# Finer places per expert in a fused attention and top-1 expert kernel: token counts rounded to 8 instead of 32

## The chip, the cores and the metric

The kernel runs on one core of a Trainium2 chip. A core has five engines that run side by side and wait for each other by semaphores: TensorE (PE in the profile; PEld is its loading of weights), VectorE (DVE), ScalarE (ACT), GpSimd (POOL) and SyncE (SP, which here only starts transfers). The metric is the time of one execution on the device in microseconds. A time is the median of several executions; before the change it is 478.34 us (three runs, 477.48 to 478.46).

## The reference

A block of decayed linear attention makes x of 3072 tokens by 512 numbers. Then each token goes to one of 8 experts, the one with the largest logit, and that expert's two-layer network gives the output row:

```python
logits = x @ w_gate
expert_idx = np.argmax(logits, axis=1)
probs = np.exp(logits - logits.max(-1, keepdims=True)); probs /= probs.sum(-1, keepdims=True) + 1e-09
gate_w = probs[np.arange(N), expert_idx]
for e in range(E):
    mask = expert_idx == e
    h = np.maximum(x[mask] @ w1[e], 0.0)              # w1[e]: 512 x 1024
    out[mask] = gate_w[mask, None] * (h @ w2[e])      # w2[e]: 1024 x 512
```

All numbers are fp32. Which token goes where is known only on the device, once its logits are there.

## The kernel before, in words

**Attention and lists.** The first part (to about 137 us) computes x in blocks of 128 tokens, writes it to a table `xs` in HBM, picks each token's expert, and writes an entry (row in `xs`, row of the output, gate) into the next free place of that expert's list in HBM (`put`, L370 to L395).

**Places.** The work for an expert is laid out before the counts are known, so it gets a fixed number of places, `CAPS`. Places that no token takes hold an entry that reads a row that counts for nothing and whose output row is skipped. Expert 0 comes first; the other seven follow in order of their counts, largest first, which the device finds out at run time (L730 to L764). This text calls them rank 1 to rank 7. `CAPS` before is three tiles of 128 and a fourth of `LASTS`: 416, 448, 416, 416, 384, 384, 384, 384. Should an expert have more tokens than places, a loop at the end (L805 to L823), behind a condition, runs further tiles with that expert's weights loaded anew.

**Passes.** `make_pass` (L405) lays out one pass: its tile widths (`m.widths`), and the load of its list. There are nine. Expert 0 has two: 0a, its first 256 places, started before attention ends, and 0b, the rest. Then one for each rank. A pass has these steps:

- `fetch` (L428): GpSimd gathers the tokens' rows, one indirect transfer a tile (L436).
- `turn` (L460): TensorE transposes the tiles, four chunks of 128 features each (L465), and VectorE and ScalarE copy them out of PSUM (L452, L450). A tile of w tokens is a transpose with w rows in and w columns out.
- First layer. Passes 0a and 0b use `hidden` (L470): 32 matmuls (L475) whose moving operand is all the pass's tokens at once. The ranks use `hidden_fast` (L542), a form of Strassen's product: the tokens are cut into two halves of h = n/2, and 56 matmuls (L551) each stream h columns; sums of halves are formed on VectorE (L488 to L492, L560) and ScalarE. `token_sums` (L534) and `first_sums`, `second_sums` (on GpSimd, L512 and L515) form the operands' sums ahead of time.
- Second layer. `outputs_fast` (L572) makes tiles 0 and 1 together in the same form (L579), and leaves the third and fourth tiles to `outputs` (L598): eight matmuls of 512 columns (L609), where a tile narrower than 128 is cut into k = 128 / w column groups of TensorE's array, each writing its own range of PSUM partitions; VectorE adds the groups' partial sums (L613 to L618).
- `scatter` (L440): GpSimd writes the rows to their places in the output.

**Order.** The loop at L777 issues, for each pass, its first layer, then the transposes and sums of the pass behind it, then its outputs. The gather of the pass after next is issued there too, and waits until a transpose has freed its buffer; the next weights are loaded once a buffer of weights is free. On every engine instructions run in the order in which they stand.

Of the kernel before, what the change touches and what calls it, by code (L numbers as in the profile page):

```python
# [20 lines left out]
def kernel(  # L21
# [29 lines left out]
    nc = tc.nc  # L51
    B, H, S, D = q.shape
    N, MD = out.shape
    E = moe_w_gate.shape[1]
    F = moe_w1.shape[2]
    P = 128
# [3 lines left out]
    DC = MD // P  # L60
    FC = F // P


    TG = 3
    NR = E - 1
    LASTS = [32, 64, 32, 32, 0, 0, 0, 0]
    CAPS = [TG * P + last for last in LASTS]

    TE = 2
    EARLY = TE * P  # L70
# [2 lines left out]
    R = N + EARLY + P  # L73
    ENTRY = 4

    MORE = -((TG * P - N - EARLY) // P)

    const = ctx.enter_context(tc.tile_pool(name="const", bufs=1))
    dram = ctx.enter_context(tc.tile_pool(name="dram", bufs=1, space=DRAM))
# [66 lines left out]
    for i in range(E):  # L146
        nc.vector.memset(caps[:, i:i + 1], float(CAPS[i]))

# [9 lines left out]
    for h in itertools.chain(range(0, H, 2), range(1, H, 2)):  # L158
        nc.vector.tensor_tensor_scan(
            out=decay[:, h % 2, h // 2, :], data0=lam_bc[:, h:h + 1].to_broadcast([P, C]),  # L160
# [11 lines left out]
    def pick(per_e, e):  # L172

        if isinstance(e, int):
            return per_e[e]
        return per_e[bass.ds(e, 1)].squeeze(0)

    def load_weights(e):
        w1t = wpool.tile([P, DC, F], F32, tag="w1", name="w1t")
        nc.sync.dma_start(out=w1t, in_=pick(w1_r, e))  # L180
        w2t = wpool.tile([P, FC, MD], F32, tag="w2", name="w2t")
        nc.sync.dma_start(out=w2t, in_=pick(w2_r, e))
        return w1t, w2t
# [11 lines left out]
    def bank(i, shape, name):  # L195
        return ps.tile(shape, F32, tag=f"bank{i}", name=name)
# [7 lines left out]
    def pin(inst):  # L204
        tc.keep_in_program_order(inst)
# [196 lines left out]
    NT = TG + 1  # L402
    by_e = slots.rearrange("(e r) c -> e r c", e=E)

    def make_pass(e, r0, tiles, last, name):  # L405

        m = SimpleNamespace(tiles=tiles, last=last, widths=[P] * tiles + [last] * (last > 0))
        src = by_e[e] if isinstance(e, int) else by_e[bass.ds(e, 1)].squeeze(0)
        m.n = sum(m.widths)
        nt = len(m.widths)  # L410
        m.list = ffn.tile([P, NT, ENTRY], F32, name=f"list_{name}", bufs=1)
        nc.sync.dma_start(
            out=m.list[:, :nt, :],
            in_=src[r0:r0 + nt * P, :].rearrange("(t p) c -> p t c", t=nt))
        m.ids = m.list.bitcast(I32)
        m.w = e
        return m

    def at(m, t):

        w = m.widths[t]
        return m.ids[:w, t, 0:1], m.ids[:w, t, 1:2], m.list[:w, t, 2:3]
# [5 lines left out]
    def fetch(m, rows=1 + N):  # L428
        m.xg = []
        for t, w in enumerate(m.widths):  # L430
            if t % 2 == 0:
                m.xg.append(ffn.tile([P, 2, MD], F32, tag="xg", name="xg", bufs=2))
            gather(m.xg[-1][:w, t % 2, :], at(m, t)[0], rows)
# [6 lines left out]
    def scatter(idx, src):  # L440

        put = nc.gpsimd.indirect_dma_start(  # L442
            out=out, out_offset=bass.IndirectOffsetOnAxis(ap=idx, axis=0), in_=src,
            in_offset=None, bounds_check=N - 1, oob_is_err=False)
        tc.declare_no_dep(put.ins, group="rows", reason="a token is on one list, once")
        tc.add_to_no_dep_group("rows", put.ins)
# [13 lines left out]
    def turn(m, pin=lambda inst: inst):  # L460
        m.xgT = ffn.tile([P, DC, m.n], F32, tag="xgT", name="xgT", bufs=1)
        for dc in range(DC):
            tp = bank(next(tp_banks), [P, m.n], "tp")
            for t, w in enumerate(m.widths):
                pin(nc.tensor.transpose(tp[:, t * P:t * P + w],  # L465
                                        m.xg[t // 2][:w, t % 2, dc * P:(dc + 1) * P],
                                        ident[:w, :w]))
            evac(dc, m.xgT[:, dc, :], tp)

    def hidden(m, w1t):  # L470
        m.hT = ffn.tile([P, FC, m.n], F32, tag="hT", name="hT", bufs=1)
        for fc in range(FC):
            ph = bank(next(ph_banks), [P, m.n], "ph")
            for dc in range(DC):
                nc.tensor.matmul(ph, lhsT=w1t[:, dc, fc * P:(fc + 1) * P], rhs=m.xgT[:, dc, :],  # L475
                                 start=(dc == 0), stop=(dc == DC - 1))
            relu(fc, m.hT[:, fc, :], ph)
# [120 lines left out]
    def outputs(m, w2t, tiles=None):  # L598
        for t in tiles or range(len(m.widths)):
            w = m.widths[t]  # L600


            k = P // w
            _, idx, gate = at(m, t)
            po = bank(next(po_banks), [P, MD], "po")

            for i, fc in enumerate((0, 1, 4, 5, 2, 3, 6, 7)):
                part = slice(i % k * w, (i % k + 1) * w)
                nc.tensor.matmul(po[part], lhsT=m.hT[:, fc, t * P:t * P + w], rhs=w2t[:, fc, :],  # L609
                                 start=(i < k), stop=(i >= FC - k), skip_group_check=True)  # L610
            o = ffn.tile([P, MD], F32, tag="o", name="o", bufs=4)
            if t % 2 or k > 1:
                nc.scalar.activation(o[:w], po[:w], ACT.Copy, scale=gate)  # L613
            else:
                nc.vector.tensor_scalar_mul(o[:w], po[:w], gate)  # L615
            for j in range(1, k):
                nc.vector.scalar_tensor_tensor(out=o[:w], in0=po[j * w:(j + 1) * w], scalar=gate,
                                               in1=o[:w], op0=ALU.mult, op1=ALU.add)  # L618
            scatter(idx, o[:w])

# [27 lines left out]
    def enter(n, b):  # L648
        if n + 1 < NSTEP:
            loaded[n + 1, b] = load(n + 1, b)  # L650
        if (n, b) == (NSTEP - 2, B - 2):
            weights.append(load_weights(0))
        m = SimpleNamespace(n=n, b=b, qT=[], qsT=[], kT=[], kd=[], mt=[], xT=[])
        m.q, m.k, m.v = loaded[n, b]

        for s, turn_one in (((0, turn_q), (1, turn_q), (0, turn_k), (1, turn_k)) if not (n or b)
                            else ((0, turn_q), (0, turn_k), (1, turn_q), (1, turn_k))):
            turn_one(m, s)
        return m
# [3 lines left out]
    def give_places(group):  # L663
        put(*group)
        if group[:2] == early:
            start_early()
# [15 lines left out]
    passes = []  # L682
    skip = const.tile([P, 1], F32, name="skip")

    def start_early():

        had = bank(5, [P, E], "had")
        pin(nc.tensor.matmul(had, lhsT=ones, rhs=acc_early, start=True, stop=True))
        nc.vector.tensor_scalar(out=skip, in0=had[:, 0:1], scalar1=-1.0, scalar2=float(EARLY),
                                op0=ALU.mult, op1=ALU.add)  # L690
        nc.vector.tensor_scalar_max(skip, skip, 0.0)
        base[0] = const.tile([P, E], F32, name="ebase_late")
        nc.vector.tensor_copy(base[0], ebase)
        nc.vector.tensor_add(base[0][:, 0:1], base[0][:, 0:1], skip)
        m = make_pass(0, 0, TE, 0, "0a")
        fetch(m, 1 + ((NSTEP - 2) * B + CUT) * C)
        passes.append(m)

    order = [(n, b) for n in range(NSTEP) for b in range(0, B, 2)]
    cur, last = enter(*order[0]), None  # L700
    for s in range(2):
        score(cur, s)
    for i in range(len(order)):
# [19 lines left out]
        last, cur = cur, ahead  # L723
# [35 lines left out]
    beyond = const.tile([P, E + 1], I32, name="beyond")  # L759
# [4 lines left out]
    nc.vector.tensor_reduce(out=beyond[:, E:], in_=beyond[:, :E], axis=AX.X, op=ALU.max)  # L764


    passes.append(make_pass(0, EARLY, TG - TE, LASTS[0], "0b"))
    for i in range(1, E):
        e = nc.values_load(turns[0:1, i:i + 1], min_val=1, max_val=E - 1,
                           engines=[mybir.EngineType.SP])  # L770
        passes.append(make_pass(e, 0, TG, LASTS[i], str(i)))
        if i == 1:
            weights.append(load_weights(e))
    for m in passes[1:3]:
        fetch(m)
    last = len(passes) - 1
# [25 lines left out]
            weights.append(load_weights(passes[i + 2].w))  # L802


    most = nc.values_load(beyond[0:1, E:E + 1], min_val=0, max_val=MORE)  # L805
    with tc.If(most > 0):
        for i in range(E):
            tiles = nc.values_load(beyond[0:1, i:i + 1], min_val=0, max_val=MORE)
            with tc.If(tiles > 0):
                e = i  # L810
                if i > 0:
                    e = nc.values_load(turns[0:1, i:i + 1], min_val=1, max_val=E - 1)
                w1t, w2t = load_weights(e)
                with tc.For_i(0, tiles, 1) as r:
                    m = SimpleNamespace(n=P, widths=[P])
                    m.list = ffn.tile([P, 1, ENTRY], F32, tag="list", name="list")
                    m.ids = m.list.bitcast(I32)
                    nc.sync.dma_start(
                        out=m.list[:, 0, :], in_=pick(by_e, e)[bass.ds(r * P + CAPS[i], P), :])
                    fetch(m)  # L820
                    turn(m)
                    hidden(m, w1t)
                    outputs(m, w2t)  # L823
# [28 lines left out]
```

## Time and profile before

| what | value |
|---|---|
| median of three runs | 478.34 us |
| the profiled execution | 478.98 us |
| its span, first to last instruction | 477.2 us |
| granted TensorE clock, mean | 0.997 |
| TensorE busy | 457.3 us, 96% |
| of it: L609, L551's first group, L579's first group | 81.1, 42.8, 26.8 us |
| share of L551, L579, L609, L475, L465 in the chain that ended last | 28%, 18%, 16%, 5%, 3% |
| VectorE, ScalarE, GpSimd busy | 47%, 27%, 52% |

How to read it: the page describes one execution. An engine's busy time is the union of its instructions. An fp32 matmul of the program leaves two records, so 56 matmuls of L551 are "x112". The chain that ended last is followed back from the last instruction, at each step to what released it. In a group, `128*128 128x192` is a weight tile of 128 rows by 128 columns against a moving operand of 128 rows by 192 columns, then follow the count, the busy time, the mean of one in ns, and the idle time before them with what ended it. A matmul's own duration holds its way through the array and overlaps the next, so the price of one in a stream is read from the chain: the length of a piece over its count.

### The profile page before, as it was taken

What the parts mean: (1) busy time and instruction counts of PE and PEld (TensorE: products, weight loads), DVE (VectorE), ACT (ScalarE), POOL (GpSimd) and SP (SyncE); (2) the same over time, 40 slices, a digit from 0 to 9 for tenths busy, and PEclk for the clock granted to TensorE, in tenths of its full rate; (3) what the DMA queues carried; (4) which work ended last, traced back from release to release, by engine and by line L of the source; (5) the groups of instructions that cost most, each with busy time, mean ns of one, the idle gap of its engine ahead of it and who ended that gap; (6) DMA issues with size and microseconds to landing.
All of it is one profiled execution on the core that took longest, in us unless ns stands there. A gap on an engine that the chain in (4) does not pass through costs nothing.

```text
span 477.2 us, 8695 instructions
## 1 busy us (share of the span) xinstructions
PE 457.3 (96%) x3468; PEld 383.1 (80%) x3468; DVE 224.4 (47%) x525; ACT 127.0 (27%) x323; POOL 247.7 (52%) x189
## 2 busy tenths in 40 slices
PE   4799999999899999999999999999999999999994
PEld 3789999998686677957994898699699689779963
DVE  3657758585450134452345436434524623753421
ACT  3364445544320111222131122113112212211310
POOL 5423644524335829849806951991694497711001
PEclk9999999999999999999999999999999999999998
DMA  9999999999318557060506152351633615001001
GB/s 170 240 243 260 217 239 216 257 305 279 101 47 320 157 193 250 32 243 33 208 13 242 36 212 87 157 199 47 243 110 132 233 39 211 0 19 44 1 17 51
DMA packets 99856, 72.84 MB, mean 153 GB/s; under 512 B 81226, under 2 KB 81230, under 8 KB 99808
## 3 DMA queue, kind: packets, MB, share of 16 engines
q1 hardware_dynamic: 88688, 51.97, 39.2%
q0 software_dynamic: 5008, 13.41, 7.8%
q10 hardware_dynamic: 6112, 6.83, 4.3%
q8 instruction: 29, 0.48, 0.5%
q14 instruction: 19, 0.16, 0.1%
HBM read 59.13 MB, written 13.40 MB: 152 GB/s over the span
## 4 chain that ended last, share of the span: by engine, by line
PE 71%; issue 3%; DVE 1%; DMA 1%; POOL 0%; POOLq 0%; ACT 0%
PE p L551 28%; PE p L579 18%; PE po L609 16%; PE ph L475 5%; PE tp L465 3%; DMA xg<-xs,list_0a 1%; DVE h_qsT L498 0%; DVE hT L560 0%; PE tx L326 0%; POOL slots L390 0%; PE tx L328 0%; DVE xgT L452 0%; PE rank L377 0%; POOLq L805 0%; ACT hT L562 0%
## 5 line engine op out<-in xcount | busy, mean ns | idle before, releaser
L609 PE MATMUL po<-w2t,hT 128*128 128x512 f32 (+2 forms) x224 | 81.1, 597 | 0.0
L436 POOL DMA_INDIRECT xg<-xs,list x24 | 26.0, 1084 | 75.7 <-PE tp L465 70.2
L609 PEld LDWEIGHTS po<-w2t,hT 128*128 128x128 f32 (+2 forms) x224 | 31.6, 169 | 37.5 <-issue 37.2
L562 ACT ACTIVATE hT<-hT 128x384 f32<-128x384 f32 (+2 forms) x56 | 30.2, 540 | 89.8 <-DVE hT L560 89.8
L442 POOL DMA_INDIRECT out_dram<-o,list x24 | 23.7, 989 | 52.0 <-DVE o L615 28.9
L551 PE MATMUL p<-xgT,w1t 128*128 128x192 f32 (+2 forms) x224 | 42.8, 334 | 0.0
L390 POOL DMA_INDIRECT slots<-entry,slot_i x24 | 23.6, 985 | 34.9 <-DVE slot_i L388 13.7
L551 PEld LDWEIGHTS p<-xgT,w1t 128*128 128x128 f32 x224 | 38.7, 190 | 1.1 <-issue 0.8
L238 POOL TENSOR_TENSOR kd<-k_in,kdec 128x512 f32<-128x512 f32 x20 | 20.4, 1042 | 26.5 <-PE cp L301 14.7
L254 DVE TENSOR_TENSOR mt<-sp,decay 128x512 f32<-128x512 f32 x48 | 29.8, 682 | 6.2 <-PE sp L248 6.1
L591 DVE SCALAR_TENSOR_TENSOR o<-p,list,o 128x256 f32<-128x256 f32 x28 | 13.5, 483 | 32.9 <-PE p L579 17.0
L579 PE MATMUL p<-w2t,hT 128*128 128x256 f32 x112 | 26.8, 382 | 0.0
L579 PEld LDWEIGHTS p<-w2t,hT 128*128 128x128 f32 x112 | 21.0, 190 | 6.9 <-issue 4.4
L248 PE MATMUL sp<-qT,kT 64*128 64x128 f32 x384 | 24.7, 278 | 0.1
L248 PEld LDWEIGHTS sp<-qT,kT 64*128 64x128 f32 x384 | 22.4, 188 | 2.2 <-issue 1.9
L284 PE MATMUL op<-mt,v_in 128*64 128x128 f32 x384 | 23.6, 274 | 0.4 <-ACT fence L280 0.4
L475 PE MATMUL ph<-xgT,w1t 128*128 128x256 f32 (+1 forms) x128 | 23.9, 342 | 0.0
L560 DVE TENSOR_TENSOR hT<-p,u_qsT 128x384 f32<-128x384 f32 (+2 forms) x28 | 16.1, 575 | 16.5 <-PE p L551 16.5
L213 PE MATMUL tq<-ident,q_in 128*128 128x128 f32 x96 | 15.4, 286 | 7.9 <-DMA q_in<-in_q_dram 6.8
L465 PEld LDWEIGHTS tp<-ident,xg 128*128 128x128 f32 (+1 forms) x112 | 13.4, 140 | 11.7 <-issue 3.6
L293 ACT COPY xT<-op 128x512 f32<-128x512 f32 x24 | 12.9, 590 | 33.6 <-PE op L272 29.8
L488 DVE TENSOR_TENSOR u_kT<-p,u_qT 128x384 f32<-128x384 f32 (+2 forms) x14 | 8.1, 576 | 29.3 <-PE p L551 29.3
(162 smaller groups left out, 968.5 us busy)
## 6 DMA issues: line engine op xcount, KB each, us to landing
w1t<-in_moe_w_dram SPq DMA_DIRECT2D x8, 2048.0 KB, 7.7
w2t<-in_moe_w_dram SPq DMA_DIRECT2D x8, 2048.0 KB, 9.1
xs<-x ACTq DMA_DIRECT2D x24, 256.0 KB, 4.8
q_in<-in_q_dram SPq DMA_DIRECT2D x11, 512.0 KB, 8.4
k_in<-in_k_dram SPq DMA_DIRECT2D x11, 512.0 KB, 8.4
v_in<-in_v_dram SPq DMA_DIRECT2D x11, 512.0 KB, 8.7
q_in<-in_q_dram SPq DMA_DIRECT2D x2, 256.0 KB, 5.9
k_in<-in_k_dram ACTq DMA_DIRECT2D x2, 256.0 KB, 5.6
```

The source lines that it names most:

```text
L248: pin(nc.tensor.matmul(sp[u][:, i, b, :], lhsT=m.kT[s][halves[u], i, b, :], rhs=m.qT[s][halves[u], i, b, :], start=(i == 0 and b == 0), st ...
L254: nc.vector.tensor_mul(mt[:, u], sp[u], decay[:, u, s * HP // 2:(s + 1) * HP // 2].unsqueeze(2).to_broadcast(shp))
L284: pin(nc.tensor.matmul(out_at(m, b, u, hp), lhsT=m.v[:, b, 2 * hp + u, :], rhs=m.mt[hp // 2][:, u, hp % 2, b, :], start=(m.n == 0 and hp = ...
L390: put = nc.gpsimd.indirect_dma_start(out=slots, out_offset=bass.IndirectOffsetOnAxis(ap=slot_i[:, i:i + 1], axis=0), in_=entry[:, n, b, :] ...
L436: nc.gpsimd.indirect_dma_start(out=dst, out_offset=None, in_=xs[:rows, :], in_offset=bass.IndirectOffsetOnAxis(ap=idx, axis=0))
L442: put = nc.gpsimd.indirect_dma_start(out=out, out_offset=bass.IndirectOffsetOnAxis(ap=idx, axis=0), in_=src, in_offset=None, bounds_check= ...
L465: pin(nc.tensor.transpose(tp[:, t * P:t * P + w], m.xg[t // 2][:w, t % 2, dc * P:(dc + 1) * P], ident[:w, :w]))
L475: nc.tensor.matmul(ph, lhsT=w1t[:, dc, fc * P:(fc + 1) * P], rhs=m.xgT[:, dc, :], start=(dc == 0), stop=(dc == DC - 1))
L551: nc.tensor.matmul(p[:, i, :], lhsT=lhs[:, dc, (c + i) * P:(c + i + 1) * P], rhs=rhs[:, dc, :], start=(dc == 0), stop=(dc == DH - 1))
L562: nc.scalar.activation(outs[i][k], outs[i][k], ACT.Relu)
L579: nc.tensor.matmul(p, lhsT=lhs[:, fc, :], rhs=rhs[:, fc, :], start=(fc == 0), stop=(fc == FC // 2 - 1))
L609: nc.tensor.matmul(po[part], lhsT=m.hT[:, fc, t * P:t * P + w], rhs=w2t[:, fc, :], start=(i < k), stop=(i >= FC - k), skip_group_check=True)
```

## The change

`CAPS` is written out, each count rounded up to a multiple of 8: 392, 424, 408, 408, 384, 368, 368, 360. `make_pass` takes the number of places and cuts it into tiles of 128 and a rest, so the third tile may be narrower than 128 (112 and 104 in ranks 5 to 7). In `outputs` the column groups no longer lie w apart but `apart`, the next power of two at least w, not under 32: widths 8 and 24 stand in four groups 32 apart, 40 in two groups 64 apart, 104 and 112 in one. `MORE`, the bound of the closing loop's count, becomes a list by expert.

```diff
-    LASTS = [32, 64, 32, 32, 0, 0, 0, 0]
-    CAPS = [TG * P + last for last in LASTS]
+    CAPS = [392, 424, 408, 408, 384, 368, 368, 360]
...
-    MORE = -((TG * P - N - EARLY) // P)
+    MORE = [-((cap - N - EARLY) // P) for cap in CAPS]
...
-    def make_pass(e, r0, tiles, last, name):
-        m = SimpleNamespace(tiles=tiles, last=last, widths=[P] * tiles + [last] * (last > 0))
+    def make_pass(e, r0, places, name):
+        m = SimpleNamespace(widths=[min(P, places - r) for r in range(0, places, P)])
...
-            k = P // w
+            apart = max(P // 4, 1 << (w - 1).bit_length())
+            k = P // apart
...
-                part = slice(i % k * w, (i % k + 1) * w)
+                part = slice(i % k * apart, i % k * apart + w)
                 nc.tensor.matmul(po[part], lhsT=m.hT[:, fc, t * P:t * P + w], rhs=w2t[:, fc, :],
                                  start=(i < k), stop=(i >= FC - k), skip_group_check=True)
...
-                nc.vector.scalar_tensor_tensor(out=o[:w], in0=po[j * w:(j + 1) * w], scalar=gate,
+                nc.vector.scalar_tensor_tensor(out=o[:w], in0=po[j * apart:j * apart + w], scalar=gate,
                                                in1=o[:w], op0=ALU.mult, op1=ALU.add)
...
-        m = make_pass(0, 0, TE, 0, "0a")
+        m = make_pass(0, 0, EARLY, "0a")
...
-    passes.append(make_pass(0, EARLY, TG - TE, LASTS[0], "0b"))
+    passes.append(make_pass(0, EARLY, CAPS[0] - EARLY, "0b"))
...
-        passes.append(make_pass(e, 0, TG, LASTS[i], str(i)))
+        passes.append(make_pass(e, 0, CAPS[i], str(i)))
```

More of the change, by code (lines that the diff above doesn't have):

```diff
@@ L802 @@
             weights.append(load_weights(passes[i + 2].w))
-    most = nc.values_load(beyond[0:1, E:E + 1], min_val=0, max_val=MORE)
+    most = nc.values_load(beyond[0:1, E:E + 1], min_val=0, max_val=max(MORE))
     with tc.If(most > 0):
         for i in range(E):
-            tiles = nc.values_load(beyond[0:1, i:i + 1], min_val=0, max_val=MORE)
+            tiles = nc.values_load(beyond[0:1, i:i + 1], min_val=0, max_val=MORE[i])
             with tc.If(tiles > 0):
```

## The prediction

> **What bounds the kernel now.** I read the page first, then the chain of waits in order of time, the groups of instructions kept apart by shape, and single stretches of time. The page's first part names the engine:
>
> ```profile
> PE 457.3 (96%) x3468; PEld 383.1 (80%) x3468; DVE 224.4 (47%) x525; ACT 127.0 (27%) x323; POOL 247.7 (52%) x189
> ```
>
> TensorE is busy 96% of the span, but that is an average, and busy is not the same as bound. The chain in order of time settles it for the expert passes (here 0b, rank 1, the start of rank 2, the outputs of rank 3 and the first half of rank 4; the x column counts profile records, two for each fp32 matmul, one for each transpose):
>
> ```profile
> 163.03 0.47 PE ph L475 x2
> 163.78 8.62 PE ph L475 x62
> 172.40 1.21 PE tp L465 x8
> ...
> 183.94 21.39 PE p L551 x112
> 205.32 1.15 PE tp L465 x8
> 206.47 1.05 PE po L609 x2
> ...
> 208.68 9.79 PE po L609 x30
> 218.47 12.28 PE p L579 x56
> 230.75 19.69 PE p L551 x112
> ...
> 294.50 0.86 PE po L609 x2
> ...
> 296.16 7.86 PE po L609 x30
> ...
> 316.31 18.20 PE p L551 x112
> 334.51 0.65 PE tp L465 x6
> ```
>
> From 163 us on each piece starts where the last ended, all on PE; the one gap is 1.1 us near 413.4, where VectorE is late with a copy out of PSUM. So a nanosecond less of PE work in a pass is a nanosecond less of time, provided that the price follows the width. It does: the 112 records of L551 take 18.20 us at 192 columns, 19.69 at 208, 21.39 at 224, i.e. 162.5, 175.8 and 191.0 ns each. From 192 to 208 that is 0.83 ns a column, and 162.5 = 2.5 + 192 x 0.833. The formula gives 175.8 at 208 (exact), 189.2 at 224 (the first pass shows 0.2 us more in all), 215.8 at 256 (L579: 12.09 / 56 = 215.9) and 429.2 at 512 (L609).
>
> **The change, part by part.** Built, the changed kernel has its instructions in the same order on every engine; only sizes differ, so nothing is moved past a queue and no wait is added. The widths in places:
>
> - 0b: 160 to 136. L475 has 64 records: 64 x 24 x 0.833 = 1.28 us.
> - rank 1: 448 to 424, halves 224 to 212. 112 x 12 x 0.833 = 1.12 us.
> - ranks 2 and 3: 416 to 408, halves 208 to 204. 112 x 4 x 0.833 = 0.37 us each, 0.75 us.
> - rank 4: stays 384. Nothing.
> - ranks 5 and 6: 384 to 368, halves 192 to 184. 112 x 8 x 0.833 = 0.75 us each, 1.49 us.
> - rank 7: 384 to 360, halves 192 to 180. 112 x 12 x 0.833 = 1.12 us.
>
> Sum 5.76 us, all on the path. 0b may give more: its 64 records took 9.09 us, 142 ns each against 135.8 by the formula; were the surplus to vanish, 0.4 us more. I take it as staying.
>
> Is the formula good below 192? PE's weight loads are what could stop it:
>
> ```profile
> 231.00:250.50 19.50, 19.50 (x113) 19.46 (x112) 7.99 (x15) 4.87 (x9) 6.17 (x4) 1.00 0.35 129
> L551 PEld LDWEIGHTS p<-xgT,w1t 128*128 128x128 f32 x224 | 38.7, 190 | 1.1 <-issue 0.8
> 132.38 0.23 PE tx L326 x2
> 132.61 0.23 PE tx L328 x2
> ```
>
> The first line is L551 of rank 2 in a table of stretches (after the length: PE, PEld, DVE, ACT, POOL busy, granted clock, DMA share, GB/s). Weight loads are busy the whole stretch at 190 ns each, longer than a 176 ns matmul; the Trainium skill ("Trainium Kernel Development and Optimization", Performance Expectations) calls the load's busy share a good metric of nearness to the limit and the matmul's a bad one. By that rule L551 is bound by loads, and narrower matmuls would give nothing below some floor. The rows decide: L326 and L328 stream 136 columns against a full 128x128 weight tile each, and take 115 ns (2.5 + 136 x 0.833 = 115.8). So loads keep up down to 136, the narrowest width that the change makes. With a floor at today's 162.5 ns (and at today's price in 0b), ranks 5 to 7 and 0b give nothing: 5.76 would be 1.87 us. I take 5.76.
>
> **Transposes (L465).** Each of the seven passes whose width changes has four partial ones, one a chunk: 0b and ranks 1 to 3 as today, ranks 5 to 7 anew. A full one costs 0.65 / 6 = 108 ns. Eight with two of 64 rows take 1.21 us before rank 1, so a partial one is (1.21 - 0.65) / 2 = 280 ns; with 32 rows 250 ns (1.15 us). The Trainium skill ("TensorEngine Tiling (Array Packing)", Key Properties) says that changing the tiling mode drains the array: these 32- and 64-row transposes do change it. 40 rows stay in the 64-row mode, 24 and 8 in the 32-row mode, so the drain stays and 24, 8 and 24 rows less save 20, 7 and 20 ns: 4 x (20 + 20 + 7 + 7) = 0.2 us. The new partial ones of 112 and 104 rows (twelve) have no row of their own. Bounds: as a full one, 13 to 20 ns less, 0.2 us saved; as today's partial ones, (250 to 280) - 108, about +0.16 each, +1.9 us. By the rule 112 rows need the 128-row mode, no switch, no drain; I take the gain, 0.2 us, and keep 1.9 for the range.
>
> **Output matmuls (L609).** A tile costs 16 records of 512 columns whatever its width, unless groups run side by side. Today: a pass with 32 wide took 0.86 + 7.86 = 8.72 us (rank 3; ranks 2 and 0b 9.1), less 16 x 0.429 = 6.87 for a full tile, leaves 1.9 to 2.3; 64 wide: 1.05 + 9.79 - 6.87 = 3.97. The new 8 and 24 wide start at partitions 0, 32, 64, 96 (four groups), 40 wide at 0 and 64 (two): as many groups at the same starts as before. The 112 and 104 wide third tiles are one group, 6.87 us as before; only weight columns go, loaded behind a 429 ns matmul. Nothing, on either side.
>
> **Off the path.** VectorE's and ScalarE's work on the halves shrinks (556 ns at 384, 592 at 416), which widens their slack. L617 and L613 on 8 to 40 partitions cost what they do on 32 (747 and 680 ns, set by 512 columns). GpSimd's gathers (L436) stay about 1 us each and as many. One rule speaks against them: the Trainium skill ("DMA: Bandwidth & Descriptors", Why a DMA increments its semaphore by 16 and not by 1) picks the largest engine count up to 16 that divides the rows, so 8, 24, 40 and 104 rows go over 8 engines, where 32, 64 and 128 went over 16. By it a 104-row gather has 13 rows an engine instead of 8, and 40 rows 5 instead of 4. From 160 to 180 us the software queue's 374 packets took 17.9% of 16 engines, 0.15 us each: +0.75 and +0.15 us of landing. No row shows such a gather. Most land tens of us before use. The tightest is rank 1's last, issued at 166.4 and used at 172.4:
>
> ```profile
> 168.00:169.00 1.00, 1.00 (x10) 1.00 (x9) 0.00 (x0) 0.30 (x1) 0.00 (x0) 1.00 0.48 139
> 169.00:170.00 1.00, 1.00 (x10) 1.00 (x9) 0.32 (x1) 0.00 (x0) 0.00 (x0) 1.00 0.00 0
> ```
>
> No data moves after 169.0, so it has 3.4 us to spare, and its issue waits for 0b's transposes at 163.8, ahead of what gets shorter. The change takes 1.3 and the rule 0.15: about 1.9 us stay. If the cover went, what is late is the transposes before rank 1, and all behind them, one for one.
>
> **The sum.** 5.76 + 0.2 + 0.2 = 6.1 us. The profiled execution took 478.98 us, span 477.2; it becomes 472.9, span 471.1. It lay 0.6 above the median of the runs, so the median goes from 478.34 to 472.2.
>
> **Rivals.**
>
> - Partial transposes of 112 and 104 rows drain too: +2.1 against the sum, 474.3. For it: every partial one today costs 250 ns or more. Against: those change the row mode.
> - Weight loads are the floor (above): gain about 2.2 us, 476.1. Against it stand L326's 115 ns.
> - A handoff turns late. The 1.1 us gap of rank 6 comes from a VectorE sum that took 1.80 us instead of 0.69 while GpSimd was adding; GpSimd starts there on PE's own progress, so I expect it to stay. A second one of its kind, or the gather above, gives 473 to 475.
> - The other side: the 8, 24 and 40 wide groups no longer run side by side. Then the narrow tile of 0b and of ranks 1 to 3 costs 6.87 us each: 27.5 against about 10.4 now, +17.1, net +11, 489. It decides from 6.1 us more on these 64 records, 95 ns each. Against it: same starts, and no group wider than its share of 32 or 64 columns.
> - The change doesn't do what it says: some expert has more tokens than places, and the closing loop runs another tile with freshly loaded weights and nothing beside it. An estimate from the rows: loads 9, gather 5, L475's 64 at 108 ns 7, outputs 7, scatter 3: over 30 us. I counted: on the reference's inputs expert 0 takes 385 (392 places), and the others by rank 418, 407, 401, 380, 364, 361, 356 (424, 408, 408, 384, 368, 368, 360). All fit, rank 2 by one.
>
> **How the numbers follow.** Forecast 0.73; drained transposes 0.10; a late handoff 0.08; load floor 0.04; groups in sequence 0.03; overflow 0.01; nothing measurable 0.01. A measurement of this kernel can tell about 0.2% (1 us) from no change. Faster: 0.95, same 0.01, slower 0.04. The range runs from 0b's surplus vanishing and a little more (471.0) to drained transposes (474.3).
>
> **What would show it.** In the profile after: L551 at 179.2 (212 columns), 172.5 (204), 155.8 (184), 152.5 ns (180) by the chain; L475 of 0b in 7.8 us; six transposes with two of 112 rows still 0.65 us, not 0.95; the narrow tiles still near 2 and 4 us; no new PE wait before rank 1. Wrong would be a rate that stays at 162.5 under 192 columns, narrow tiles of 6.9 us in 0b or ranks 1 to 3, or any matmul after the last pass.

## The result, and the profile after

The changed kernel takes 472.95 us (median of four runs, 471.71 to 473.74) against 478.40 before on the same chip (four runs, 477.48 to 479.92): ratio 0.989, 95% interval 0.986 to 0.992. The prediction was 472.2 in 471.0 to 474.3.

Line numbers of the changed kernel are one or two lower: L549 is the first layer's L551, L473 is L475, L463 is L465, L577 is L579, L589 is L591, L496 is L498, L608 is L609. The profile's first part, engines busy:

```profile
PE 452.1 (96%) x3468; PEld 377.5 (80%) x3468; DVE 222.5 (47%) x525; ACT 125.7 (27%) x323; POOL 247.6 (53%) x189
```

As many instructions as before on each engine, 5.2 us less on TensorE, GpSimd unchanged. The chain that ended last, in order of time, from 0b on:

```profile
160.36 1.14 PE tp L463 x6
161.50 0.43 PE ph L473 x2
162.19 7.38 PE ph L473 x62
169.58 1.17 PE tp L463 x8
...
172.98 8.04 PE po L608 x30
181.01 20.26 PE p L549 x112
...
226.67 19.32 PE p L549 x112
...
269.66 19.32 PE p L549 x112
...
350.05 17.45 PE p L549 x112
367.50 0.64 PE tp L463 x6
...
426.88 17.08 PE p L549 x112
443.96 6.87 PE po L608 x16
450.82 12.10 PE p L577 x56
462.95 0.49 DVE o L589
```

Piece by piece against before: 0b 9.09 to 7.81 us; rank 1 21.39 to 20.26; ranks 2 and 3 19.69 to 19.32; rank 5 18.20 to 17.45; rank 7 18.20 to 17.08. For rank 6 both chains show 104 of the 112 records, 16.91 and 16.22 us, because behind the 104th they leave TensorE for the late copy; scaled to 112 that is 0.74 less. Together 1.28 + 1.13 + 0.74 + 0.75 + 0.74 + 1.12 = 5.76 us, the sum of the prediction. That it agrees to the hundredth is chance, as each row is rounded to a hundredth. Transposes add about 0.3, and from 0b's first transpose to the end of the last matmul the way went from 308.7 us (161.82 to 470.50) to 302.6 (160.36 to 462.95): 6.1 us less. TensorE is idle for 1.13 us of it, all but a little of that in the gap behind rank 6 (before: 307.58 of 308.68 us busy):

```profile
160.36:462.95 302.59, 301.46 (x1537) 247.18 (x1535) 132.79 (x240) 62.98 (x130) 174.30 (x102) 1.00 0.34 120
```

The spans differ by more, 477.2 to 469.8. Ahead of 0b lie 1.46 us (161.82 against 160.36), in the first part, where the two kernels do the same work; behind the last matmul 0.15 us are lost. That part moves from run to run and from chip to chip, so below a whole-run median is always set beside a stretch of the trace that leaves it out: from the start of rank 1's first layer to the end of the last matmul, where the VectorE instruction that waits for it starts (before 183.94 to 470.50, 286.56 us; changed 181.01 to 462.95, 281.94 us, 4.62 less). Without 0b, the prediction's sum for this stretch is 4.7.

### The profile page after: what moved, and what is told of

The parts are those of the page before. It is cut to its first block, busy times and chain, and to the rows that moved or that the text cites. A ratio compares the mean times of both kernels' runs of the same rounds, so it can differ in the third digit from the quotient of the medians.

```text
span 469.8 us, 8695 instructions
## 1 busy us (share of the span) xinstructions
PE 452.1 (96%) x3468; PEld 377.5 (80%) x3468; DVE 222.5 (47%) x525; ACT 125.7 (27%) x323; POOL 247.6 (53%) x189
## 4 chain that ended last, share of the span: by engine, by line
PE 93%; DMA 3%; DVE 1%; ACT 1%; ACTq 0%; issue 0%; POOLq 0%; POOL 0%
PE p L549 27%; PE p L577 18%; PE po L608 17%; PE sp L246 5%; PE ph L473 5%; PE op L282 4%; PE tp L463 3%; PE tx L324 3%; PE cp L299 2%; PE op L270 2%; PE tx L326 2%; PE tk L211 2%; PE tq L211 2%; DMA back<-in_moe_w_gate_dram 2%; DMA k_in<-in_k_dram 1%; PE rank L375 1%
## 5 line engine op out<-in xcount | busy, mean ns | idle before, releaser
L608 PE MATMUL po<-w2t,hT 128*128 128x512 f32 (+5 forms) x224 | 81.0, 596 | 0.0
L608 PEld LDWEIGHTS po<-w2t,hT 128*128 128x128 f32 (+5 forms) x224 | 30.6, 162 | 38.2 <-issue 37.9
L560 ACT ACTIVATE hT<-hT 128x408 f32<-128x408 f32 (+4 forms) x56 | 29.5, 527 | 86.7 <-DVE hT L558 86.7
L549 PE MATMUL p<-xgT,w1t 128*128 128x204 f32 (+4 forms) x224 | 41.5, 328 | 0.0
L549 PEld LDWEIGHTS p<-xgT,w1t 128*128 128x128 f32 x224 | 37.6, 190 | 1.2 <-issue 0.9
L589 DVE SCALAR_TENSOR_TENSOR o<-p,list,o 128x256 f32<-128x256 f32 x28 | 13.6, 484 | 32.9 <-PE p L577 17.0
L577 PE MATMUL p<-w2t,hT 128*128 128x256 f32 x112 | 26.8, 382 | 0.0
L577 PEld LDWEIGHTS p<-w2t,hT 128*128 128x128 f32 x112 | 21.1, 190 | 7.0 <-issue 4.5
L558 DVE TENSOR_TENSOR hT<-p,u_qsT 128x408 f32<-128x408 f32 (+4 forms) x28 | 15.7, 561 | 15.8 <-PE p L549 15.8
L473 PE MATMUL ph<-xgT,w1t 128*128 128x256 f32 (+1 forms) x128 | 22.6, 332 | 0.0
L282 PEld LDWEIGHTS op<-mt,v_in 128*64 128x64 f32 x384 | 20.7, 137 | 1.2 <-ACT fence L278 0.9
L463 PEld LDWEIGHTS tp<-ident,xg 128*128 128x128 f32 (+3 forms) x112 | 13.3, 140 | 10.1 <-issue 3.8
```

Source lines behind the costliest of these rows:

```text
L282: pin(nc.tensor.matmul(out_at(m, b, u, hp), lhsT=m.v[:, b, 2 * hp + u, :], rhs=m.mt[hp // 2][:, u, hp % 2, b, :], start=(m.n == 0 and hp = ...
L463: pin(nc.tensor.transpose(tp[:, t * P:t * P + w], m.xg[t // 2][:w, t % 2, dc * P:(dc + 1) * P], ident[:w, :w]))
L549: nc.tensor.matmul(p[:, i, :], lhsT=lhs[:, dc, (c + i) * P:(c + i + 1) * P], rhs=rhs[:, dc, :], start=(dc == 0), stop=(dc == DH - 1))
L560: nc.scalar.activation(outs[i][k], outs[i][k], ACT.Relu)
L577: nc.tensor.matmul(p, lhsT=lhs[:, fc, :], rhs=rhs[:, fc, :], start=(fc == 0), stop=(fc == FC // 2 - 1))
```

## Experiments

The kernel before took 477.64 us beside the first four runs (chip A), 488.30 beside the next four (chip B, where the first part was slower in every trace taken there: the changed kernel's rank 1 begins at 189.4 instead of 181.0), and 477.61 beside the last three (chip C).

### Do the parts add up?

Ranks 5 to 7 alone:

```diff
-    CAPS = [392, 424, 408, 408, 384, 368, 368, 360]
+    CAPS = [416, 448, 416, 416, 384, 368, 368, 360]
```

> Only ranks 5 to 7 get fewer places (368, 368, 360); 0b and ranks 1 to 3 keep 160, 448, 416, 416. Price follows the width: 1.49 + 1.12 us on the first layer and 0.2 on the transposes, 2.8 us less than before, 475.6. If weight loads set a floor at 162.5 ns: no change. If the partial transposes of 112 and 104 rows drain the array: 0.7 us less, about 477.7.

Measured 474.86 us (ratio 0.9941, 0.9922 to 0.9960), 2.78 below before. 0b and ranks 1 to 3 alone:

```diff
-    CAPS = [392, 424, 408, 408, 384, 368, 368, 360]
+    CAPS = [392, 424, 408, 408, 384, 384, 384, 384]
```

> Only 0b and ranks 1 to 3 get fewer places (136, 424, 408, 408); ranks 5 to 7 keep 384. Price follows the width: 1.28 + 1.12 + 0.75 us and 0.2 on the transposes, 3.3 us less than before, 475.1. With this run and the one on ranks 5 to 7 the parts should add up to the whole change (6.1); if a handoff took part of it, they would not.

Measured 473.63 us (0.9922, 0.9898 to 0.9945), 4.0 below before, 0.7 more than expected. The stretch from rank 1 on tells whether that is the edit. The first fence is from the chain of the run with ranks 5 to 7 alone, the second from the other:

```profile
182.84 21.38 PE p L549 x112
...
353.82 17.45 PE p L549 x112
371.28 0.64 PE tp L463 x6
...
430.67 17.08 PE p L549 x112
...
466.74 0.49 DVE o L589
```

```profile
180.77 20.27 PE p L549 x112
...
349.82 18.20 PE p L549 x112
...
428.19 18.20 PE p L549 x112
...
465.38 0.49 DVE o L589
```

The stretch is 283.90 us in the first (2.66 less than before; 2.8 were expected, 0.2 of it of transposes, which gave about 0.05) and 284.61 in the second (1.95 less; 1.12 + 0.75 and 0.1 of transposes were expected). 2.66 + 1.95 = 4.61, and the whole change took 4.62 from it. The parts add up, no handoff took a share, and the surplus 0.7 us of the second median lies outside the stretch: 0b begins at 160.12 in the second run and at 160.72 in the first, on the same chip.

### How far down does the price follow the width?

The closing loop is taken out and places are cut below the tokens, so that some tokens go unprocessed:

```diff
-    CAPS = [392, 424, 408, 408, 384, 368, 368, 360]
+    CAPS = [392, 424, 352, 328, 320, 288, 272, 264]
...
-    most = nc.values_load(beyond[0:1, E:E + 1], min_val=0, max_val=max(MORE))
...
```

> Is there a floor under which the price of a matmul no longer follows its width? The changed kernel with places 392, 424, 352, 328, 320, 288, 272, 264 and without the closing loop, so tokens beyond the places of ranks 2 to 7 are left out. Only L551's place in the code counts: by 2.5 + h x 0.833 ns a record it takes 179 (h = 212), 149.2 (176), 139.2 (164), 135.8 (160), 122.5 (144), 115.8 (136) and 112.5 ns (132). If weight loads bound it, the price stops falling somewhere between 180, the narrowest seen, and 132. Transposes: 96 and 72 rows (ranks 2 and 3) cost as a full one if the 128-row mode is what matters (six with two partial: 0.60 to 0.64 us), 64 rows and fewer (ranks 4 to 7) about 250 to 280 ns each (six with two partial: 0.9 to 1.0 us). If being partial is what costs, ranks 2 and 3 show 0.9 us too.

The time, 434.16 us, says little, as tokens are missing. The chain, with the transposes of the rank behind each first layer:

```profile
201.15 0.61 PE tp L463 x6
...
225.27 16.71 PE p L549 x112
241.98 0.57 PE tp L463 x6
...
262.18 15.59 PE p L549 x112
277.76 0.99 PE tp L463 x6
...
279.77 0.70 PE tp L463 x6
...
298.71 15.21 PE p L549 x112
313.93 0.94 PE tp L463 x6
...
332.55 13.72 PE p L549 x112
346.27 0.91 PE tp L463 x6
...
363.09 10.21 PE p L549 x88
```

Over their counts the pieces give 149.2 ns at 176 columns, 139.2 at 164, 135.8 at 160, 122.5 at 144 and 116.0 at 136; rank 7's groups of eight start 0.90 us apart, 112.5 ns at 132. Every one is 2.5 + h x 0.833 within 0.2 ns. There is no floor down to 132, though the weight loads were as good as always busy in this layer. The 160-column row also shows that 0b's 142 ns at 160 is not a matter of width.

The transposes: six with two partial ones take 0.61 us at 96 rows and 0.57 at 72, less than six full ones (0.65), but 0.99 at 64, 0.94 at 32 and 0.91 at 16. Being partial costs nothing at 72 rows and more. At 64 and fewer a transpose between full ones costs 130 to 170 ns more than a full one ((0.99 - 0.43) / 2 - 0.11 at 64 rows, where 0.43 are the four full ones). The second six transposes of that rank were issued with the two 64-row ones behind one another, and took 0.70 us where full ones take 0.80. The weight loads of the two sixes:

```profile
277.91 0.40 PEld L463 LDWEIGHTS tp<-ident,xg 64*128 64x128 f32 x3 [0.17 <-issue]
278.48 0.14 PEld L463 LDWEIGHTS tp<-ident,xg 64*128 64x128 f32 x1 [0.17 <-issue]
...
280.13 0.20 PEld L463 LDWEIGHTS tp<-ident,xg 64*128 64x128 f32 x2 [0.17 <-issue]
```

Idle time of 0.17 us stands ahead of each change to 64 rows, not ahead of each transpose. (The row of three takes in full ones between.) So the price seems to be one of changing; no run was made with the order alone changed.

Ahead of rank 7 the price finds another bound. The timeline of VectorE there:

```profile
376.12 6.82 DVE L496 TENSOR_TENSOR h_qsT<-hT 128x512 f32<-128x512 f32 x1 [0.50 <-ACT hT L560]
```

This sum takes 0.69 us elsewhere. Here it stands 6.82, through three sums of GpSimd (L513, 375.4 to 382.5), and TensorE waits 5.4 us for the copy behind it. It is the same wait as in the 1.1 us gap, five times as long.

### The rival on the other side

```diff
-            apart = max(P // 4, 1 << (w - 1).bit_length())
+            apart = P
```

> The changed kernel with every narrow tile's output matmuls in one column group (apart = 128): what the rival on the other side would have done. Third and fourth tiles of 8, 24 and 40 tokens cost 16 x 0.429 = 6.87 us each instead of about 2 (8 and 24) and 4 (40): 17.1 us more than the changed kernel, 490. If groups did not run side by side in the changed kernel, there would be no difference from it (472.9). VectorE's sums over groups fall away, which costs or gives nothing.

Measured 490.07 us (one run). The chain of this run, outputs of 0b and of ranks 1, 2 and 3 but for their first two records:

```profile
172.84 13.17 PE po L608 x30
...
209.61 13.20 PE po L608 x30
...
257.75 13.18 PE po L608 x30
...
304.85 12.99 PE po L608 x30
```

The changed kernel has 8.04, 9.77, 8.05 and 7.86 there: 5.13, 3.43, 5.13 and 5.13 more, 18.8 us. So the groups do run side by side at 8, 24 and 40 columns: four take 6.87 - 5.13 = 1.74 us, two 6.87 - 3.43 = 3.44. The prediction's 1.9 to 2.3 for a narrow tile had taken a little of the transposes between the pieces along with it, hence 17.1.

### The price of a place too few

```diff
-    CAPS = [392, 424, 408, 408, 384, 368, 368, 360]
+    CAPS = [392, 424, 400, 408, 384, 368, 368, 360]
```

> The changed kernel with 400 places for rank 2, which has 407 tokens, so that the closing loop runs one tile: the price of a count that does not fit. The estimate in the prediction was over 30 us, so 503 or more; the rank's own narrower tile saves about 0.4 us. If the closing loop were cheap or overlapped, under 10 us.

Measured 522.74 us (one run), 45 above the kernel before on that chip and about 51 above what the changed kernel would take there (477.6 less 6.1). The list's transfer from its chain, then stretches, columns as in the prediction:

```profile
466.31 13.16 DMA list<-slots
...
463.00:484.00 21.00, 0.44 (x3) 0.04 (x1) 0.48 (x1) 0.00 (x0) 2.56 (x3) 0.56 0.67 239
484.00:488.00 4.00, 3.67 (x16) 3.30 (x17) 0.58 (x2) 0.53 (x2) 0.00 (x0) 0.50 0.00 0
488.00:494.00 6.00, 6.00 (x50) 6.00 (x49) 1.08 (x4) 0.83 (x3) 0.00 (x0) 0.88 0.00 0
502.00:521.00 19.00, 0.00 (x0) 0.00 (x0) 0.31 (x1) 0.00 (x0) 1.01 (x1) 0.62 0.03 9
```

TensorE stands for 20 us: the list's transfer, issued behind 4 MB of weights, lands 13.2 us later, and only then can the gather start. The granted clock is 0.50 over the 4 us that follow, so the first matmuls run at half speed. And 17 us pass after the last transfer is issued, until the program ends (5 in the changed kernel); what fills them was not looked into. The estimate (over 30) had no term for the list's wait behind the loads, for the clock or for the ending.

### Rounding to 2, and the gap ahead of rank 7

```diff
-    CAPS = [392, 424, 408, 408, 384, 368, 368, 360]
+    CAPS = [386, 418, 408, 402, 380, 364, 362, 356]
```

> Places rounded to 2 instead of 8: 386, 418, 408, 402, 380, 364, 362, 356. The halves become 209, 204, 201, 190, 182, 181 and 178 columns, so the second halves start at odd multiples of 4 and 8 bytes. If only the width is paid: 64 x 6 x 0.833 in 0b and 112 x (3 + 0 + 3 + 2 + 2 + 3 + 2) x 0.833 in the ranks, 0.32 + 1.40 = 1.7 us less than the changed kernel. If a start that is no multiple of 16 bytes slows the stream, L551 lies above 2.5 + h x 0.833 in ranks 1, 3, 4, 5, 6 and 7 and not in rank 2, and the run is no faster than the changed kernel.

and, apart from it, the first copy of rank 7's transposes on ScalarE (`evac` with an odd number):

```diff
-            evac(dc, m.xgT[:, dc, :], tp)
+            evac(1 if getattr(m, "late", False) and dc < 2 else dc, m.xgT[:, dc, :], tp)
...
     last = len(passes) - 1
+    passes[last].late = True
```

> The changed kernel with the first copy of rank 7's transposes out of PSUM moved from VectorE to ScalarE, so that it doesn't stand behind the sum that GpSimd holds up. If that sum alone makes the 1.1 us gap of PE between rank 6 and rank 7, the gap goes and the run is 1.1 us below the changed kernel. If the sums behind it are late for L579 instead, the gap comes back ahead of L579 and nothing is gained.

> Places rounded to 2 and the copy on ScalarE together: 1.7 + 1.1 = 2.8 us below the changed kernel, 8.9 below the kernel before, if both hold and are independent.

> The changed kernel as it is, beside the three below on one chip. By the sum of the prediction 6.1 us less than before.

| chip | kernel | median, us | ratio to before (95%) | rank 1 to last matmul, us |
|---|---|---|---|---|
| B | changed | 479.93 | 0.9852 (0.9818 to 0.9886) | 281.93 |
| B | rounded to 2 | 478.77 | 0.9818 (0.9788 to 0.9847) | 280.64 |
| B | copy on ScalarE | 482.31 | 0.9867 (0.9826 to 0.9909) | 280.62 |
| B | both | 478.39 | 0.9807 (0.9771 to 0.9843) | 279.30 |
| C | copy on ScalarE | 470.43 | 0.9860 (0.9839 to 0.9880) | 280.63 |
| C | both | 468.44 | 0.9810 (0.9794 to 0.9826) | 279.29 |

By the medians on chip B rounding gives 1.2 us and both edits 1.5, of the 1.7 and 2.8 expected; the copy costs 2.4 us by the median and saves 1.3 by the stretch. In its profile rank 1 begins at 192.34, 2.9 us after the changed kernel's 189.40, and the edit touches nothing before rank 7. The traces of chip B show where the first part is slow: the chain stands 5.4 us near 110 us on something that the profile does not name, and the granted clock from 110 to 150 us is 0.96 in the changed kernel and 0.91 in the copy on ScalarE, where it is 1.00 in the changed kernel's first trace and in the copy's trace on chip C. Runs on another chip were to tell which is right:

> The two edits together once more, since the first part of the kernel moved by several us from run to run: 8.9 us below the kernel before in the median; in the trace, from the start of rank 1's first layer to the end of the last matmul, 2.6 us less than the changed kernel, as in the earlier run.

> The copy on ScalarE alone once more: 1.1 to 1.3 us below the changed kernel in the stretch from rank 1 on, 7.2 to 7.4 below the kernel before in the median. If the edit really costs time ahead of rank 1, as the earlier medians had it (482.31 against 479.93), it lies above the changed kernel again.

On chip C the copy is 7.18 us below before and both are 9.17 below, as expected (7.2 to 7.4, and 8.9); the stretches repeat to 0.01 us. The chain of the copy on ScalarE (chip C) where the gap was:

```profile
387.95 17.45 PE p L549 x112
405.41 0.62 PE tp L463 x6
406.03 0.87 PE po L608 x2
406.89 0.62 PE tp L463 x6
407.52 6.02 PE po L608 x14
413.53 12.09 PE p L577 x56
```

Nothing stands between the pieces any more. In this run VectorE's sum L496 still takes 1.83 us; it only no longer stands in front of the copy.

Rounding to 2 saves 1.29 us of the 1.40 expected in this stretch. L549 takes 20.02 us at 209 columns, 19.07 at 201, 18.04 at 190, 17.29 at 182 and 16.91 at 178, which is 170.3 ns at 201 where the formula has 170.0. So halves whose second one starts at an odd multiple of 4 or 8 bytes cost 0.1 to 0.3 ns a record more, and no more than that. Whether it is the start or the odd width itself, this run cannot tell. The two edits together are the fastest kernel here, 468.44 us; but with 418, 380, 364 and 356 places for as many tokens, one token more brings the 51 us of the run above.

## Why the prediction was right, and where it was off

- **The bound.** Right: from 0b on TensorE has no gap to speak of but the one behind rank 6 (near 413 before, near 407 after), and 5.76 us less work on it, with 0.3 of transposes, gave 6.1 us.
- **The first layer.** 5.76 forecast, 5.76 found. The rates said for the profile after were 172.5, 155.8 and 152.5 ns at 204, 184 and 180 columns, and are 172.5, 155.8 and 152.5; at 212 the formula's 179.2 was 180.9, because rank 1's surplus of 0.2 us stayed, as it had been at 224. 0b's surplus stayed too: 7.81 us against the 7.8 forecast. What causes either surplus stays open.
- **Weight loads.** The rule that their busy share tells the limit would have made it 2.2 us. The trace spoke against it, and the run over widths did down to 132 columns.
- **Transposes.** 112 and 104 rows cost as full ones (0.64 us for six with two of them); forecast 0.4 us in all, found about 0.3. The price of 250 to 280 ns, read as that of a partial transpose, seems to be that of changing to 64 rows or fewer and back; the forecast holds either way, as the order of the transposes did not change.
- **Output matmuls.** 8, 24 and 40 columns still run side by side; the rival's price was 18.8 us instead of 17.1.
- **Gathers.** Rank 1's last gather was issued at 165.6, no data moved after 168.0, and its transposes began at 169.6: 1.6 us to spare against the 1.9 forecast. It took 2.4 us to the last data where the 64-row one had taken 2.6 (166.4 to 169.0). The prediction applied the rule that it cites wrongly: the largest count up to 16 that divides 24, 40 and 104 is 12, 10 and 13, not 8, so a 40-row gather has 4 rows an engine, as one of 64 rows has, and a 104-row gather 8, as one of 128. The 0.15 and 0.75 us more do not follow from it. The one gather fits that, but how many engines it went over was not read from a trace.
- **The gap ahead of rank 7.** Expected to stay, and it did (1.1 us). That GpSimd's sums are its origin was a reading of the trace; shown is that a copy that no longer stands behind the held-up sum removes it.
- **From the span to the median.** The step from 6.1 us to the whole run is the loosest: 5.45 us between the first medians (478.40, 472.95), 8.4 on chip B, where the changed kernel's stretch from rank 1 on is the same as in its first trace to 0.01 us. That the first median came within 0.8 us of the forecast owes something to luck. What moves the first part was not tried.

## To carry to other kernels

Where one engine's work lies end to end, take a price per column from two shapes in the chain of the trace, check it on a third, and an edit of widths can be forecast to a tenth of a microsecond; whether a smaller shape has a floor is best read from another line that already runs at that shape. Compare small edits over a stretch of the trace that leaves out what they don't touch: a median misjudged the copy on ScalarE by 3.7 us, sign included. Here a cut of padding paid down to single columns in the first layer; in the third and fourth tiles it paid nothing for the output matmuls as long as the number of groups stayed the same. A count with no place to spare should be weighed against the price of the way out.

## What the runs showed of the hardware that was not expected

- While GpSimd adds from SBUF, a VectorE sum of two SBUF operands can stand for the whole of it: 6.82 us instead of 0.69 through three GpSimd sums, 1.83 through the end of one. That one waits for the other is read from the times; no run moved the GpSimd sums.
- Idle time of TensorE is paid twice: after 20 us without work the granted clock was 0.50 for 4 us and 0.88 over the next 6.
- A transpose of 64 rows or fewer between full ones cost 240 to 280 ns instead of 108, one of 72 rows or more nothing extra; two 64-row ones behind one another cost less.
- A moving operand of odd width, whose second half starts at an odd multiple of 4 bytes, streams as fast as others, but for 0.3 ns a record.
